# Lists of token numbers with 64 bytes for each slot, scattered and copied whole

## The chip, the cores and the metric

One core of a Trainium2 chip runs one program. The metric is the time on the device of one execution, in microseconds (us). Its engines are TensorE (PE, matmuls and transposes), VectorE (DVE), ScalarE (ACT), GpSimd (POOL) and SyncE (SP, which issues most of the transfers); PEld is TensorE's loading of weights. Transfers are carried by 16 DMA engines.

## The reference

Three layers follow one another, all in fp32:

- attention over 4 batches of 8 heads, 576 tokens, 64 wide, with keys and values averaged over groups of 8 (so 72 keys). It gives x, 2304 tokens of 512;
- a mixture of 8 experts: each token goes to the expert with the largest of 8 logits, x·w_gate. An expert takes the first 576 tokens that come to it, in order of their numbers; for those y = relu(x·w1)·w2 (512 to 1024 to 512), scaled by the softmax weight; other tokens give 0;
- a last layer for all 2304 tokens: g = s·relu(x·w_in)² + b, then g·w_out (512 to 2048 to 512).

## The kernel before, in words

**Routing.** Attention runs in tiles of up to 128 tokens, five in each batch. `route` (L296) follows behind it for a batch, or for a part of it: for each token it works out the slot (`rsi`) that the token has in its expert's part of a list, and POOL then scatters the numbers of the tokens (`tok`, from an iota, L360) into the list `ids` in DRAM, one number of 4 bytes to each slot, by an indirect DMA of up to 128 numbers for every tile (L363; 20 in all, five for a batch; those of the last batch come as three and two). `scale` (L283) stores the rows of x to the DRAM array `xd` (L294). Before the first scatter, `fill` (L841) writes `ids` and the second list, `idc`, full with a number that is out of bounds.

**Units.** The tokens are worked on in units: 288 slots of one expert each, then two small ones of 144, and the last of the big units is wide (288 and 64 more). The first two units begin while attention still runs for the last batches. For a unit u, SP reads where its slots begin (`values_load`), loads their token numbers `idt` (L809, 96 partitions of 3), then weights: `kraw` for w1 (L787) and `vraw` for w2 (L793). POOL gathers the rows of x by `idt` (L804). The weights are split in a high and a low part, since a product is made of three matmuls: ACT casts the high part (`w1h` L796, `w2h` L800), POOL or DVE subtracts for the low part (`w1l` L797, `w2l` L801). `x_part` (L811 on) transposes x on PE and splits it (`xs`, ACT L816 and DVE L817), `layer1` (L824 on) and `layer2` (L998) multiply.

**The list of results.** `store_y` (L1000) stores y of a unit to `yt`, and then copies the unit's token numbers from `idt` in SBUF into `idc` (L1004), at the place where its results lie; the small units do so from `ids_s`, and the wide one's last 64 numbers come from `idw` (L1143). When the units are done, `last_layers` (L1240) reads y and, by `load_y` (L908), the numbers `it`, works the last layer out for 256 tokens at a time and scatters the rows of the output by `it` (L1325). It begins with the cast `gh` (L1312) and the loads of `sb` (L1464), of `wo` and of `raw` (spilled weights `wi`, L932).

**What sets the order.** The program's order is written out by hand on every engine, and each engine's queue runs in order. SP issues its transfers one after the other; eight semaphores are used in turn for them, so a DMA on SP waits for the one eight before it to have landed. POOL's transfers have eight of their own. Tiles that take the place of others in SBUF wait for all that was done with those: the pools `one` (attention) and `left` (kept to the end) matter below. When attention is over, the pool `one` is given up, and the tiles of the units (`w2h` for f from 1 on among them) take its place.

Of the kernel before, what the change touches and what calls it, by code (L numbers as in the profile page):

```python
# [10 lines left out]
I32 = mybir.dt.int32  # L11
# [7 lines left out]
B, H, S, D = 4, 8, 576, 64  # L19
T = B * S  # L20
DM = H * D
E, FF, FF2 = 8, 1024, 2048
POOL = 8
SP = S // POOL
P = 128
NB = 5
VW = D + 1 + E
G = H + H // 2
BIG = 1 << 17
KSCALE = 1.0 / (POOL * 8.0)  # L30
CH = 288
SUB = 96
# [2 lines left out]
KF = FF // P  # L35
KF2 = FF2 // P
CU = 256
TINY = float(np.array([897 << 20], np.int32).view(np.float32)[0])


# [39 lines left out]
def attention(nc, tc, c, a, cap, capp, left, big, xd, ids, run, hist, first, ps0):  # L80
# [3 lines left out]
    with ExitStack() as es:  # L84
        one = es.enter_context(tc.tile_pool(name="a1", bufs=1))
# [191 lines left out]
        todo, routes, scales, at_pe = [], [], [], [None]  # L277
# [18 lines left out]
        def route(b, t0, t1):  # L296

            g, w = b % 2, t1 - t0
            l = lg[g][:, t0:t1]
            bc = lambda z: z.unsqueeze(2).to_broadcast([P, w, E])  # L300
            tmp = lambda name, shape, dt=F32: left.tile([P, NB] + shape, dt, name=f"{name}{len(routes) % 2}")[:, 0:w]
# [4 lines left out]
            d = tmp("rd", [E])  # L306
# [49 lines left out]
            yield  # L356
            si = tmp("rsi", [], I32)
            nc.vector.tensor_copy(si, sf)
            tok = tmp("tok", [], I32)
            nc.gpsimd.iota(tok, pattern=[[P, w]], base=b * S + t0 * P, channel_multiplier=1)  # L360
            for t in range(w):
                n = rows(t0 + t)
                i = nc.gpsimd.indirect_dma_start(out=ids, out_offset=bass.IndirectOffsetOnAxis(ap=si[:n, t:t + 1], axis=0),  # L363
                                                 in_=tok[:n, t:t + 1], in_offset=None, bounds_check=E * capp - 1, oob_is_err=False)
                tc.declare_no_dep(i.ins, group="scatter", reason="slots of different tokens")
                tc.add_to_no_dep_group("scatter", i.ins)
            if t1 == NB and b:
# [24 lines left out]
        o = ps1.tile([P, 2, 512], F32, name="o")  # L392
# [90 lines left out]
        while todo or scales:  # L483
            more = 7
            while more and todo:
                more -= 1
                if step():
# [3 lines left out]
                    o = ps1.tile([P, 2, 512], F32, name="o")  # L491
# [14 lines left out]
SM = CH // 2  # L506
SSUB = SM // 2
# [8 lines left out]
MORE = 64  # L516
# [237 lines left out]
class Experts:  # L754
# [51 lines left out]
                                          bounds_check=rows - 1, oob_is_err=False)  # L806

    def load_ids(self, u, slots):
        self.nc.sync.dma_start(out=self.idt[u % 3], in_=slots.rearrange("(s p) o -> p (s o)", p=SUB))  # L809

    def x_part(self, u, k, p, v=None):  # L811
        v = v or self.v
# [28 lines left out]
    def fill(self, pool):  # L841

        nc = self.nc
        for d, w in ((self.ids, E * self.capp // SUB + 1), (self.idc, (T + 2 * CH) // SUB)):
            z = pool.tile([SUB, w], I32, name=f"z{w}")
            nc.gpsimd.iota(z, pattern=[[1, w]], base=BIG, channel_multiplier=0)
            nc.sync.dma_start(out=d.rearrange("(p n) o -> p (n o)", p=SUB), in_=z)

    def beside(self, i, pool):

# [57 lines left out]
    def load_y(self, u):  # L908
        nc = self.nc
        nc.sync.dma_start(out=self.yr, in_=self.yt[:, u * CU:u * CU + CU].rearrange("(k p) n -> p k n", p=P))  # L910
        nc.sync.dma_start(out=self.it[u % 4], in_=self.idc[u * CU:u * CU + CU].rearrange("(j p) o -> p (j o)", p=P))

    def split_y(self, k, eng):
        self.nc.scalar.copy(self.yh[:, k], self.yr[:, k])
# [21 lines left out]
    def main(self, left, one, ps):  # L936
# [44 lines left out]
        regs = self.regs  # L981
# [15 lines left out]
                for i, (l, r) in enumerate(((w2h, v.hh), (w2h, v.hl), (w2l, v.hh))):  # L997
                    nc.tensor.matmul(py[d][:, :v.n], lhsT=l[f][:, d * P:d * P + P], rhs=r[f], start=f == 0 and i == 0, stop=f == KF - 1 and i == 2)  # L998

        def store_y(u, y, ids, n, sub):  # L1000
            for d in range(KD):
                nc.scalar.copy(y[:, d], py[d][:, :n])
            nc.sync.dma_start(out=self.yt.rearrange("(d p) n -> p d n", p=P)[:, :, cols(u, n)], in_=y)
            nc.sync.dma_start(out=self.idc[cols(u, ids.shape[1] * sub)].rearrange("(s p) o -> p (s o)", p=sub), in_=ids)  # L1004

        def store_unit(u, v=self.v):
            store_y(u, yo(0 if v is wide else u % 2, v.n), self.idt[u % 3], v.n, SUB)

        pos = [0]

# [8 lines left out]
        def next_tokens(u):  # L1019
            if u < NU:  # L1020
                load_regs(u, u - 2)
                self.load_ids(u, self.ids[bass.ds(regs[u][1], CH)])
                nc.sync.dma_start(out=idw[u % 3], in_=self.ids[CH:][bass.ds(regs[u][1], MORE)])

        def tokens(u, s):
            if s < NSUB:
# [73 lines left out]
        def small_ids(s):  # L1100
            if s < E:
                load_regs(sid(s), self.t.NV + s)
                nc.sync.dma_start(out=self.ids_s[s % 4], in_=self.ids[bass.ds(regs[sid(s)][1], SM)].rearrange("(s p) o -> p (s o)", p=SSUB))

        def small_gather(s):
            for j in range(2):
# [20 lines left out]
                nc.tensor.matmul(py[d][:, :SM], lhsT=self.w2r[:, f, d * P:d * P + P], rhs=hs[f], start=f == 0, stop=f == KF - 1)  # L1127

        def store_small(s):
            store_y(sid(s), yo(s % 2, SM), self.ids_s[s % 4], SM, SSUB)  # L1130

        def next_small(s):
            if s < E:
# [3 lines left out]
        def to_small(u, v=self.v, f0=0):  # L1137

            if u == 1:
                zeros()  # L1140
            small_gather(0)
            if v is wide:
                nc.sync.dma_start(out=self.idc[CH:][cols(u, MORE)], in_=idw[u % 3])  # L1143
            with if_new(self.t.NV):
                self.load_w1(w1s(sid(0)))
            small_gather(1)
            for f in range(f0, KF):
                layer2(f, v)
                if 0 <= f - max(f0, 3) < KD:
                    small_x(0, f - max(f0, 3))  # L1150
                conv(2, MARK)
                if f == max(f0, 2):
                    with if_new(self.t.NV):
                        for j in range(0, KF, 2):
                            self.load_w2(w2s(sid(0)), j)
            store_unit(u, v)
            small_layer1(MARK)
            conv(MARK - pos[0], MARK)
# [308 lines left out]

def program(nc, tc, a, cap, out):
    capp = (-(-cap // CH) + 1) * CH
    with ExitStack() as es:  # L1470
        left = es.enter_context(tc.tile_pool(name="c", bufs=1))
        dr = es.enter_context(tc.tile_pool(name="dr", bufs=1, space=DRAM))
        xd = dr.tile([T, DM], F32, name="xd")
        ids = dr.tile([E * capp + SUB, 1], I32, name="ids")
        idc = dr.tile([T + 2 * CH, 1], I32, name="idc")
        yt = dr.tile([DM, T + 2 * CU], F32, name="yt")
        wi = [dr.tile([P, DM], F32, name=f"wi{i}") for i in range(PRE)]
        hist = left.tile([P, E], F32, name="hist")
        run = left.tile([P, E], BF16, name="run")
        ps0 = es.enter_context(tc.tile_pool(name="ps0", bufs=1, space=PSUM))  # L1480
        c = constants(nc, left, capp)
        with tc.manual_schedule():
            with tc.tile_pool(name="m", bufs=1, side="right") as m:
                x = Experts(nc, tc, c, a, left, m, xd, ids, idc, yt, wi, hist, cap, capp)
                ps = attention(nc, tc, c, a, cap, capp, left, m, xd, ids, run, hist, x, ps0)
                w = es.enter_context(tc.tile_pool(name="w", bufs=1))
                pp = es.enter_context(tc.tile_pool(name="ps", bufs=1, space=PSUM))
                ps = ps + [pp.tile([P, 512], F32, name=f"bank{i}") for i in range(2, 8)]
                with tc.tile_pool(name="m1", bufs=1) as m1:
                    x.main(w, m1, ps)  # L1490
            pool = es.enter_context(tc.tile_pool(name="n", bufs=1))
            last_layers(nc, tc, c, a, pool, x, ps, out)
# [20 lines left out]
```

## Time and profile before

| | |
|---|---|
| median of 3 runs | 694.91 us (692.51 to 697.27) |
| the profiled execution | 693.31 us, its span 691.6 us |
| PE | busy 597.8 us, 86% |
| DVE | 384.4 us, 56% |
| POOL | 328.3 us, 47% |
| ACT | 253.0 us, 37% |
| mean granted TensorE clock | 0.93 of full speed |
| transfers | 67,826 packets, 86.24 MB, 30,732 of the packets under 512 bytes |

The span is the time from the first to the last instruction of the core; the rest of an execution's time lies around it. In the rows, times are in microseconds from the span's start; "x3" is a count of instructions that the view puts together, and [4.99 <-DMA kraw<-...] says that the engine stood idle for 4.99 us before the row and what ended that. DMA is the mean busy share of the 16 DMA engines, beside the bytes that they moved.

The attention stage lies at 0 to 125 us, the routing's last scatters and the first units at 110 to 175, the units up to 370, and the last layer fills the rest.

### The profile page before, as it was taken

How to read it: one execution, taken by the hardware profiler on the slowest of the kernel's cores; microseconds unless marked ns; L12 is line 12 of the kernel's file. 1: busy time of each engine (PE TensorE's matmuls, PEld its weight loads, DVE VectorE, ACT ScalarE, POOL GpSimd, SP SyncE). 2: the span in 40 equal slices, each digit the busy share in tenths (PEclk: the TensorE clock that was granted, in tenths of full speed). 3: DMA queues.
4: the chain of work that ended last, by engine and by line, in shares of the span. 5: the costliest groups of instructions: out<-in, count | busy, mean ns of one | idle time of the engine just before them, and what ended most of it. 6: DMA issues, size and time to landing. Idle time of an engine off the chain costs nothing. (4 is left out here: it accounts for less than half of the span.)

```text
span 691.6 us, 11294 instructions
## 1 busy us (share of the span) xinstructions
PE 597.8 (86%) x3943; PEld 556.4 (80%) x3943; DVE 384.4 (56%) x804; ACT 253.0 (37%) x617; POOL 328.3 (47%) x357
## 2 busy tenths in 40 slices
PE   7788887765896898977879789999979999999986
PEld 6777876665896797977769769989859989899886
DVE  4789898865698584566353769597302112022060
ACT  1354574441554362614234744403303304124040
POOL 5566743656482552734112666455253515326081
PEclk8799998996899899998789979999989999999999
DMA  8999875875448968699851910010730100100000
GB/s 171 194 180 161 139 116 168 184 243 194 57 130 161 285 133 304 130 309 254 272 119 43 363 62 1 1 31 1 267 113 17 31 32 1 46 17 2 17 18 20
DMA packets 67826, 86.24 MB, mean 125 GB/s; under 512 B 30732, under 2 KB 38924, under 8 KB 67724
## 3 DMA queue, kind: packets, MB, share of 16 engines
q1 hardware_dynamic: 59596, 63.52, 36.7%
q0 software_dynamic: 7280, 21.51, 11.9%
q8 instruction: 43, 0.70, 0.5%
q14 instruction: 59, 0.48, 0.3%
q10 hardware_dynamic: 848, 0.02, 0.1%
HBM read 66.14 MB, written 19.72 MB: 124 GB/s over the span
## 5 line engine op out<-in xcount | busy, mean ns | idle before, releaser
L1317 PE MATMUL bank<-wo,gh 128*128 128x512 f32 (+1 forms) x448 | 132.6, 380 | 1.2 <-DVE wo L1283 1.2
L1313 POOL TENSOR_TENSOR gl<-rt,gh 128x256 fp32r<-128x256 f32 (+1 forms) x112 | 90.9, 820 | 79.9 <-ACT gh L1312 76.8
L1317 PEld LDWEIGHTS bank<-wo,gh 128*128 128x128 f32 x448 | 82.5, 193 | 15.5 <-DVE wo L1283 1.5
L1317 PE MATMUL bank<-wo,gl 128*128 128x512 f32 (+1 forms) x224 | 85.4, 381 | 4.1 <-POOL gl L1313 4.1
L998 PE MATMUL bank<-hs,w2h 128*128 128x288 f32 (+1 forms) x308 | 74.5, 332 | 8.8 <-issue 8.8
L797 POOL TENSOR_TENSOR w1l<-kraw,w1h 128x512 fp32r<-128x512 f32 x40 | 53.2, 1350 | 36.8 <-ACT w1h L796 36.6
L998 PEld LDWEIGHTS bank<-hs,w2h 128*128 128x128 f32 x308 | 56.2, 212 | 9.5 <-issue 9.3
L1324 DVE SCALAR_TENSOR_TENSOR raw<-bank,sb,c_u 128x512 f32<-128x512 f32 (+1 forms) x14 | 9.8, 710 | 96.5 <-PE bank L1317 96.5
L998 PE MATMUL bank<-hs,w2l 128*128 128x288 f32 (+1 forms) x148 | 48.3, 326 | 10.9 <-POOL w2l L801 8.9
L1307 ACT ACTIVATE rt<-tq 128x256 f32<-128x256 f32 (+1 forms) x26 | 9.6, 369 | 129.1 <-PE tq L921 105.9
L1317 PEld LDWEIGHTS bank<-wo,gl 128*128 128x128 f32 x224 | 43.0, 192 | 12.4 <-POOL gl L1313 4.6
L1308 DVE SCALAR_TENSOR_TENSOR rt<-bank,rt 128x256 f32<-128x256 f32 (+1 forms) x60 | 24.3, 405 | 44.8 <-ACT rt L1307 44.6
L1325 POOL DMA_INDIRECT out_dram<-raw,it x12 | 12.1, 1004 | 71.2 <-DVE raw L1324 58.9
L1312 ACT CAST gh<-rt 128x256 fp32r<-128x256 f32 (+1 forms) x112 | 43.1, 385 | 6.6 <-DMA idc<-ids_s 5.4
L998 PEld LDWEIGHTS bank<-hs,w2l 128*128 128x128 f32 x148 | 31.6, 214 | 11.6 <-POOL w2l L801 9.2
L921 PE MATMUL bank<-yhl,w2h 128*128 128x256 f32 x208 | 38.0, 283 | 0.0
L921 PE MATMUL bank<-yhl,w1h 128*128 128x256 f32 x208 | 37.7, 281 | 0.0
L1307 ACT ACTIVATE rt<-bank 128x256 f32<-128x256 f32 (+1 forms) x60 | 22.2, 370 | 37.4 <-PE bank L921 33.4
L921 PEld LDWEIGHTS bank<-yhl,w1h 128*128 128x128 f32 x208 | 32.3, 188 | 1.0 <-issue 0.7
L921 PEld LDWEIGHTS bank<-yhl,w2h 128*128 128x128 f32 x208 | 32.7, 191 | 0.3
L801 DVE TENSOR_TENSOR w2l<-vraw,w2h 128x512 fp32r<-128x512 f32 x39 | 28.2, 723 | 3.3 <-ACT w2h L800 2.7
L921 PE MATMUL bank<-yhl,w1l 128*128 128x256 f32 x104 | 29.3, 282 | 0.6 <-issue 0.6
(376 smaller groups left out, 1592.6 us busy)
## 6 DMA issues: line engine op xcount, KB each, us to landing
kraw<-in_moe_w_dram SPq DMA_DIRECT2D x12, 1024.0 KB
vraw<-in_moe_w_dram SPq DMA_DIRECT2D x16, 512.0 KB
c_raw<-in_moe_w_in_dram POOLq DMA_DIRECT2D x16, 512.0 KB, 9.0
kraw<-in_k_dram SPq DMA_DIRECT2D x8, 576.0 KB
out_dram<-c_u SPq DMA_DIRECT2D x1, 4608.0 KB
q<-in_q_dram SPq DMA_DIRECT2D x16, 256.0 KB
xd<-xr SPq DMA_DIRECT2D x16, 256.0 KB
vraw<-in_moe_w_dram SPq DMA_DIRECT2D x4, 1024.0 KB
```

The lines of the kernel that those rows point to most:

```text
L797: eng.tensor_sub(self.w1l[:, i], self.w1(i), self.w1h[:, i])
L801: eng.tensor_sub(self.w2l[i], self.w2r[:, i], self.w2h[i])
L921: self.nc.tensor.matmul(p[:, :CU], lhsT=l[:, k], rhs=r[:, k], start=n == 0, stop=n == 3 * KD - 1)
L998: nc.tensor.matmul(py[d][:, :v.n], lhsT=l[f][:, d * P:d * P + P], rhs=r[f], start=f == 0 and i == 0, stop=f == KF - 1 and i == 2)
L1307: nc.scalar.activation(r, p, AF.Relu)
L1308: nc.vector.scalar_tensor_tensor(out=r, in0=p, scalar=0.0, in1=r, op0=ALU.max, op1=ALU.mult)
L1312: nc.scalar.copy(gh[:, f, :n], rt[f % 4][:, :n])
L1313: nc.gpsimd.tensor_sub(gl[:, f, :n], rt[f % 4][:, :n], gh[:, f, :n])
L1317: nc.tensor.matmul(p[:, c], lhsT=l[:, f, j * P:j * P + P], rhs=wo[f][:, z, c], start=f == 0 and i == 0, stop=f == KF2 - 1 and i == 2)
L1324: nc.vector.scalar_tensor_tensor(out=o[:, c], in0=p[:, c], scalar=sb[:, 0:1], in1=sums["drop"][:, c], op0=ALU.mult, op1=ALU.add)
L1325: i = nc.gpsimd.indirect_dma_start(out=dst, out_offset=bass.IndirectOffsetOnAxis(ap=ids, axis=0), in_=o[:, c], in_offset=None, bounds_chec ...
```

## The change

`ids` and `idc` become arrays with a row of 16 numbers, 64 bytes, for each slot (`ROW`). The iota writes each token's number 16 times over, the scatter copies whole rows of 64 bytes, and whoever reads the numbers into SBUF takes the first of each row. The list arrays are rounded up to a multiple of 768 rows, so `ids` has 7680 rows of 64 bytes (it had 7008 numbers of 4 bytes) and `idc` has 3072 (it had 2880 numbers); `fill` writes both with one tile of 96 x 128 numbers. The copy of a unit's numbers no longer starts from `idt`, `ids_s` or `idw` in SBUF: it goes from `ids` to `idc` in DRAM, in one run without gaps (`store_ids`). And `tok` is taken from the pool `one` instead of `left`.

```
+ROW = 16
...
-            tok = tmp("tok", [], I32)
-            nc.gpsimd.iota(tok, pattern=[[P, w]], base=b * S + t0 * P, channel_multiplier=1)
+            tok = one.tile([P, NB, ROW], I32, name=f"tok{len(routes) % 2}")[:, 0:w]
+            nc.gpsimd.iota(tok, pattern=[[P, w], [0, ROW]], base=b * S + t0 * P, channel_multiplier=1)
             for t in range(w):
                 n = rows(t0 + t)
                 i = nc.gpsimd.indirect_dma_start(out=ids, out_offset=bass.IndirectOffsetOnAxis(ap=si[:n, t:t + 1], axis=0),
-                                                 in_=tok[:n, t:t + 1], in_offset=None, bounds_check=E * capp - 1, oob_is_err=False)
+                                                 in_=tok[:n, t], in_offset=None, bounds_check=E * capp - 1, oob_is_err=False)
...
     def load_ids(self, u, slots):
-        self.nc.sync.dma_start(out=self.idt[u % 3], in_=slots.rearrange("(s p) o -> p (s o)", p=SUB))
+        self.nc.sync.dma_start(out=self.idt[u % 3], in_=slots[:, 0:1].rearrange("(s p) o -> p (s o)", p=SUB))
...
-        for d, w in ((self.ids, E * self.capp // SUB + 1), (self.idc, (T + 2 * CH) // SUB)):
-            z = pool.tile([SUB, w], I32, name=f"z{w}")
-            nc.gpsimd.iota(z, pattern=[[1, w]], base=BIG, channel_multiplier=0)
-            nc.sync.dma_start(out=d.rearrange("(p n) o -> p (n o)", p=SUB), in_=z)
+        z = pool.tile([SUB, 8 * ROW], I32, name="z")
+        nc.gpsimd.iota(z, pattern=[[0, 8 * ROW]], base=BIG, channel_multiplier=0)
+        for d in (self.ids, self.idc):
+            d = d.rearrange("(p n k) o -> p n (k o)", p=SUB, k=8)
+            nc.sync.dma_start(out=d, in_=z.unsqueeze(1).to_broadcast(list(d.shape)))
...
-        nc.sync.dma_start(out=self.it[u % 4], in_=self.idc[u * CU:u * CU + CU].rearrange("(j p) o -> p (j o)", p=P))
+        nc.sync.dma_start(out=self.it[u % 4], in_=self.idc[u * CU:u * CU + CU, 0:1].rearrange("(j p) o -> p (j o)", p=P))
...
-        def store_y(u, y, ids, n, sub):
+        def store_ids(u, n, i=0):
+            row = lambda z: z.rearrange("(a n) o -> a (n o)", a=1)
+            nc.sync.dma_start(out=row(self.idc[i:][cols(u, n)]), in_=row(self.ids[i:][bass.ds(regs[u][1], n)]))
+
+        def store_y(u, y, n, slots):
             for d in range(KD):
                 nc.scalar.copy(y[:, d], py[d][:, :n])
             nc.sync.dma_start(out=self.yt.rearrange("(d p) n -> p d n", p=P)[:, :, cols(u, n)], in_=y)
-            nc.sync.dma_start(out=self.idc[cols(u, ids.shape[1] * sub)].rearrange("(s p) o -> p (s o)", p=sub), in_=ids)
+            store_ids(u, slots)
...
             if v is wide:
-                nc.sync.dma_start(out=self.idc[CH:][cols(u, MORE)], in_=idw[u % 3])
+                store_ids(u, MORE, CH)
...
-        ids = dr.tile([E * capp + SUB, 1], I32, name="ids")
-        idc = dr.tile([T + 2 * CH, 1], I32, name="idc")
+        ids = dr.tile([up(E * capp + SUB), ROW], I32, name="ids")
+        idc = dr.tile([up(T + 2 * CH), ROW], I32, name="idc")
```

No engine's order changes, but for one iota less in `fill` and a few instructions that work out addresses; shapes and waits do. Two places show it. The first is SP behind the loads for unit 2 and at the end of unit 0; `idt_163` are unit 2's numbers, `idw` the further 64 that a wide unit would take. Before:

```order
L809 DMA idt_163<-ids 96x3x1 [waits DMAHW5_49,DMASW4_49]
L1023 ISA
L1023 DMA idw_1877<-ids 64x1 [waits DMAHW6_49,PE_49]
L1003 REGISTER_ALU
L1003 DMA yt<-yo 128x4x288 [waits DMAHW7_49,Activation_49]
L1004 REGISTER_ALU
L1004 DMA idc<-idt_161 96x3x1 [waits DMAHW0_49]
```

With the change:

```order
L810 DMA idt_163<-ids 96x3x1 [waits DMAHW5_49,DMASW4_49]
L1031 ISA
L1031 DMA idw_1875<-ids 64x1 [waits DMASW5_49,DMASW3_49,DMASW6_49,DMASW2_49,DMASW7_49,DMASW1_49,DMAHW6_49,DMASW0_49,PE_49]
L1011 REGISTER_ALU
L1011 DMA yt<-yo 128x4x288 [waits DMAHW7_49,Activation_49]
L1006 ISA
L1006 DMA idc<-ids 16x288 [waits DMAHW0_49]
```

The copy stands where it stood, as 16 rows of 288 numbers instead of 96 partitions of 3, and it reads the list `ids` and no tile of SBUF. The load of `idw` now also waits for POOL's transfers (DMASW0 to 7).

The second place is ACT at the end of unit 0's first layer, where `w2h` of the units' own tiles is cast for the first time. Before:

```order
L826 ACTIVATE hs<-tq 128x288 [waits PE_49]
L826 ACTIVATE hs<-misc 128x288 [waits PE_49]
L800 CAST w2h<-vraw 128x512 [waits DMAHW4_49,DMAHW3_49,DMAHW5_49,DMAHW2_49,DMAHW6_49,DMAHW0_49,DMAHW7_49,DVE_49,Activation_49]
L800 CAST w2h<-vraw 128x512 x2
L796 CAST w1h<-kraw 128x512 [waits DMAHW7_49,Pool_49]
```

With the change:

```order
L827 ACTIVATE hs<-tq 128x288 [waits PE_49]
L827 ACTIVATE hs<-misc 128x288 [waits PE_49]
L801 CAST w2h<-vraw 128x512 [waits DMASW6_49,DMASW7_49,DMASW5_49,DMAHW0_49,DMASW4_49,DMAHW2_49,DMASW3_49,DMAHW3_49,DMASW2_49,DMAHW4_49,DMASW1_49,DMAHW5_49,DMASW0_49,DMAHW6_49,DVE_49,DMAHW7_49,Activation_49,Pool_49]
L801 CAST w2h<-vraw 128x512 x2
L797 CAST w1h<-kraw 128x512 [waits DMAHW7_49]
```

The first cast of `w2h` waited for transfers of SP's queue (the DMAHW semaphores: stores of x out of the same place in SBUF); it now waits for all eight of POOL's (DMASW) and for POOL itself too, since `tok` lies in the pool whose place the tile takes. These transfers are the scatters, the last of which stand on POOL ahead of the first `w2l` (L801).

## Rows read from the trace of the kernel before

**Rows 1.** The page, part 1: busy time, share of the span, instructions.

```profile
PE 597.8 (86%) x3943; PEld 556.4 (80%) x3943; DVE 384.4 (56%) x804; ACT 253.0 (37%) x617; POOL 328.3 (47%) x357
```

**Rows 2.** The chain that ended last: start, length, what; its first long piece.

```profile
401.37 2.28 POOL yhl L915 x2
```

**Rows 3.** SP's waits: line, releaser, us in total, times, longest.

```profile
SPq L809 <- DMA ids<-tok,rsi: 17.8, 2, 11.9
...
SPq L809 <- DMA idc<-idt: 7.9, 2, 4.3
...
SPq L1143 <- DMA idc<-idt: 7.4, 1, 7.4
...
SPq L1464 <- DMA idc<-ids_s: 4.1, 1, 4.1
```

**Rows 4.** Tiles ids (scatters of numbers), then it (scatters of output rows of 2 KB).

```profile
DMA to landing us min/median/max: 5.6/10.0/15.3
...
DMA to landing us min/median/max: 2.7/2.8/4.7
```

**Rows 5.** Windows: length, busy time of engines, PE clock, DMA share, GB/s.

```profile
36.00:40.00 4.00, 2.77 (x16) 2.54 (x17) 3.61 (x9) 2.94 (x7) 1.15 (x1) 0.75 1.10 140
210.00:218.00 8.00, 7.88 (x59) 7.88 (x60) 5.13 (x11) 4.63 (x11) 2.26 (x3) 1.00 1.08 97
372.00:376.00 4.00, 3.37 (x29) 3.28 (x29) 0.00 (x0) 0.00 (x0) 0.00 (x0) 1.00 0.00 0
```

**Rows 6.** POOL's timeline, 96 to 176: start, length, line, operation, idle before.

```profile
98.90 0.92 POOL L363 DMA_INDIRECT ids<-tok,rsi  x1 [0.30 <-issue]
...
128.52 0.91 POOL L363 DMA_INDIRECT ids<-tok,rsi  x1 [0.30 <-issue]
...
144.27 0.99 POOL L804 DMA_INDIRECT xg<-xd,idt  x1 [9.83 <-DMA idt<-ids]
...
156.76 0.92 POOL L363 DMA_INDIRECT ids<-tok,rsi  x1 [0.31 <-issue]
```

**Rows 7.** SP's timeline, 96 to 176 and 280 to 330.

```profile
110.70 0.37 SPq L809 DMA_DIRECT2D idt<-ids  x1
...
141.35 0.35 SPq L809 DMA_DIRECT2D idt<-ids  x1
...
293.33 1.16 SPq L787 DMA_DIRECT2D kraw<-in_moe_w_dram  x2
```

**Rows 8.** ACT's timeline, 96 to 176 and 344 to 408.

```profile
116.64 1.14 ACT L796 CAST w1h<-kraw 128x512 fp32r<-128x512 f32 x2 [4.99 <-DMA kraw<-in_moe_w_dram]
...
147.04 1.66 ACT L800 CAST w2h<-vraw 128x512 fp32r<-128x512 f32 x3 [1.65 <-DMA xd<-xr]
...
376.35 0.41 ACT L1312 CAST gh<-rt 128x256 fp32r<-128x256 f32 x1 [5.43 <-DMA idc<-ids_s]
```

**Rows 9.** PE's timeline, around the four waits that the text speaks of.

```profile
119.28 0.46 PE L243 MATMUL te<-ident,s 64*128 64x64 f32 x4 [3.90 <-ACT eT L246]
...
159.28 0.61 PE L998 MATMUL bank<-hs,w2l 128*128 128x288 f32 x1 [8.93 <-POOL w2l L801]
...
310.73 0.34 PE L1114 MATMUL tq<-ident,xg 72*128 72x72 f32 x2 [3.82 <-DVE yr L1115]
...
399.49 0.58 PE L921 MATMUL tq<-yhl,w1h 128*128 128x256 f32 x1 [4.65 <-ACT yhl L914]
```

**Rows 10.** DVE's timeline, at five places.

```profile
128.92 5.55 DVE L325 TENSOR_SCALAR rgs<-rgs 128x3 f32<-128x3 f32 x1
...
147.75 0.69 DVE L801 TENSOR_TENSOR w2l<-vraw,w2h 128x512 fp32r<-128x512 f32 x1 [1.86 <-ACT w2h L800]
...
155.22 0.16 DVE L650 TENSOR_TENSOR u_key<-u_oth,u_e 128x8 f32<-128x8 f32 x1
...
163.00 0.46 DVE L817 TENSOR_TENSOR xs<-misc,xs 128x288 fp32r<-128x288 f32 x1 [7.62 <-ACT xs L816]
...
308.57 0.43 DVE L740 TENSOR_SCALAR c_f<-c_raw 128x512 int32<-128x512 int32 x1 [6.41 <-DMA wi<-c_f]
```

More of the change, by code (lines that the diff above doesn't have):

```diff
@@ L1003, in store_y @@
             nc.sync.dma_start(out=self.yt.rearrange("(d p) n -> p d n", p=P)[:, :, cols(u, n)], in_=y)
-            nc.sync.dma_start(out=self.idc[cols(u, ids.shape[1] * sub)].rearrange("(s p) o -> p (s o)", p=sub), in_=ids)
+            store_ids(u, slots)
         def store_unit(u, v=self.v):
-            store_y(u, yo(0 if v is wide else u % 2, v.n), self.idt[u % 3], v.n, SUB)
+            store_y(u, yo(0 if v is wide else u % 2, v.n), v.n, CH)
         pos = [0]
@@ L1022, in next_tokens @@
                 self.load_ids(u, self.ids[bass.ds(regs[u][1], CH)])
-                nc.sync.dma_start(out=idw[u % 3], in_=self.ids[CH:][bass.ds(regs[u][1], MORE)])
+                nc.sync.dma_start(out=idw[u % 3], in_=self.ids[CH:][bass.ds(regs[u][1], MORE)][:, 0:1])
         def tokens(u, s):
@@ L1102, in small_ids @@
                 load_regs(sid(s), self.t.NV + s)
-                nc.sync.dma_start(out=self.ids_s[s % 4], in_=self.ids[bass.ds(regs[sid(s)][1], SM)].rearrange("(s p) o -> p (s o)", p=SSUB))
+                nc.sync.dma_start(out=self.ids_s[s % 4], in_=self.ids[bass.ds(regs[sid(s)][1], SM)][:, 0:1].rearrange("(s p) o -> p (s o)", p=SSUB))
         def small_gather(s):
@@ L1129, in store_small @@
         def store_small(s):
-            store_y(sid(s), yo(s % 2, SM), self.ids_s[s % 4], SM, SSUB)
+            store_y(sid(s), yo(s % 2, SM), SM, SM)
         def next_small(s):
@@ L1469, in program @@
     capp = (-(-cap // CH) + 1) * CH
+    up = lambda n: -(-n // (8 * SUB)) * 8 * SUB
     with ExitStack() as es:
```

## The prediction

> **What bounds the kernel now.** I began with the busy times. PE is busy for 597.8 us of the 691.6 [rows 1], so it is the bound wherever nothing holds it up, and the change takes no matmul away. A gain can only come out of PE's waits. The chain of waits, read second, says how far to look: its first long piece is POOL's `yhl` at 401.37 [rows 2], and what comes after is the last layer on PE. So the question is how much earlier the units reach 401.
>
> Third, SP's waits, since SP issues the weights in order and whatever holds it holds them. Four of its entries belong to the two lists [rows 3]: 17.8 us in two waits for scatters to land, 7.9 and 7.4 for an earlier copy into `idc`, 4.1 for the last such copy.
>
> Fourth, why these wait so long. A scatter of 128 numbers of 4 bytes needs 10.0 us at the median until it has landed, 15.3 at most; one of 128 output rows of 2 KB, issued by POOL in the same way, 2.8 [rows 4]. The one that moves fewer bytes is over three times slower. In the windows, 210 to 218 lies inside such a copy into `idc`: the DMA engines are busy throughout (share 1.08) and move 97 GB/s [rows 5], so small writes hold up the other transfers too.
>
> Fifth, the timelines, for what follows on each wait:
>
> - Batch 1's last scatter ends its issue at 98.90 + 0.92 = 99.82 [rows 6], and `idt` is loaded at 110.70 [rows 7]: 10.9 us. Weights queue behind it; ACT waits 4.99 for them [rows 8], and behind ACT PE 3.90 [rows 9].
> - Batch 2's ends at 129.43 [rows 6], `idt` for unit 1 is loaded at 141.35 [rows 7]: 11.9 us. POOL stands still for 9.83 before its gather at 144.27, and in its order the last scatters come after that; the last one ends at 157.68 [rows 6]. `w2l` is behind it, and PE waits 8.93 us for that, until 159.28 [rows 9]. The transposes behind give DVE its `xs` at 163.00, after 7.62 us of idling [rows 10].
> - The wide unit: SP's 7.4 us end in `kraw` at 293.33 [rows 7]. DVE waits 6.41 for a store to land and PE 3.82 behind it, until 310.73 [rows 10, 9].
> - The end of the units: from 372 to 376 the DMA engines move nothing [rows 5]; ACT's first `gh` waits 5.43 for the last copy to `idc` [rows 8], SP's load of `sb` 4.1 [rows 3]. PE pays later, with 4.65 at 399.49 [rows 9].
>
> **The change, part by part.**
>
> *Scatters of 64 bytes.* The same 20 DMAs, issued in about 1 us each as now. No row shows a write of 64 bytes. The ends are 2.8 us (2 KB rows) and 10.0 (4 bytes). I take 4 us, near the lower end: the two rows differ only in the size of a row, more bytes take less time there, so what is paid for is the small write, and 64 bytes are sixteen times the slow one.
>
> The first stage gives up to 3.90 (PE's wait); I pass 3.5 on to all that comes after. The second `idt` load then comes 3.5 + (11.9 - 4.9) = 10.5 earlier (4 to land, 0.9 until SP goes on), at 130.9. The gather follows 2.9 us behind it, as now (144.27 - 141.35), at 133.8. From the gather to the end of the last scatter POOL needs 157.68 - 144.27 = 13.4: 147.2, and that has landed at 151.2.
>
> *The new wait.* ACT's first `w2h` of the units' own tiles now waits for that landing. Today it starts at 147.04 [rows 8], so here the change takes back: 151.2 is 4.2 later. Behind it on ACT are two more casts, then `w1h`; POOL's `w2l` needs them, and PE the `w2l`. DVE's `w2l` starts 0.71 after ACT's cast (147.75), and DVE needs 155.38 - 147.75 = 7.6 us to finish what lies before `xs` [rows 10]. So `xs` comes 0.7 + 7.6 = 8.3 after ACT's cast: 159.5 instead of 163.00, and DVE, not POOL, is late next. The stretch up to 175 gives 3.5 us, where PE's two waits alone would have promised 12.8. Bounds: 0, and 8.93 if DVE's table work is overtaken too.
>
> *The copies.* Now: 288 writes of 4 bytes each. With the change: 16 runs of 1152 bytes in DRAM. No row shows a copy inside DRAM; the ends are 2.8 and 10.0 again [rows 4], and I take 3, since 1152 bytes are nearest to the 2 KB row. SP's 7.4 then goes and `kraw` comes 7.4 earlier; the spill's store, which DVE waits for, no longer queues behind those loads. PE's 3.82 bounds it: I take 2.5. Where the other copies are followed by loads, PE has no wait for weights that I could name, and I count nothing; PE's own work hides them.
>
> *The end of the units.* SP's 4.1 and ACT's 5.43 go: the casts no longer wait for a store that reads a tile whose place they take. Loads start 4 us earlier, and the stretch behind them waits for loads; I take 4, between 0 and 5.43.
>
> *The fill.* 7680 and 3072 rows of 64 bytes are 688,128 bytes instead of 39,552. At the 140 GB/s of 36 to 40 [rows 5] that is 4.6 us more on engines that are fully busy then. Ends 0 and 4.6. I take 1: only loads for later tiles queue behind it.
>
> *At no cost:* readers still fetch single numbers of 4 bytes, as many as before; an iota writes 80 numbers a partition instead of 5 and runs on POOL while scatters wait; the extra address instructions on SP precede DMAs that no engine awaits.
>
> Sum: -3.5 - 2.5 - 4 + 1 = -9.0. The profiled execution's 693.31 becomes 684.3. It lies 1.6 below the median of the runs, 694.91, so I say **686**. About 1% (6.95 us) is what a measurement of this kernel can tell from no change.
>
> **The rivals.**
>
> *Writes of 64 bytes land as slowly as those of 4* (slower). Then nothing shortens the chain up to the last scatter at 157.68, it lands at 167.7, and the new wait holds ACT until then. `xs` follows at 176.0 instead of 163.00: +13.0. The copies, in longer runs, still give 2.5 + 4, the fill takes 1: 694.9 + 13.0 - 6.5 + 1 = 702.4, and up to 706 if the fill costs its 4.6. It decides from the point where the last scatter lands after 163.0 - 8.3 = 154.7; as the landing enters the sum about 2.7 times ((167.7 - 151.2)/(10 - 4)), that is a landing of 5.3 us, a little below the fastest of today's, 5.6 [rows 4]. For it: the new wait is certain. Against it: the step from 10.0 to 2.8. The Trainium skill (DMA: Bandwidth & Descriptors, Specifications) says that transfers below 512 bytes are done by read-modify-write, which would put 64 bytes with the 4; by that rule the time would be this rival's. The rows bear the rule out at 4 bytes only. Chance 0.13.
>
> *The new wait eats the stage's gain* (no change). A landing near 5.3 us, or POOL's subtractions slowing DVE (DVE's L325, on 128 x 3 numbers, took 5.55 us at 128.92 [rows 10]), leaves 0 up to 175; the wide unit's 2.5 may then be hidden by DVE's own work. With 4 from the end and 1 for the fill: 692. Chance 0.25.
>
> *More than I count* (larger gain). PE's whole 8.93 goes, 3.82 and 5.43 too, and the fill is free: 694.9 - 18.2 = 677. For it: the share of 1.08 at 97 GB/s shows that the small writes stall transfers that I count at nothing. Against it: the new wait, and DVE next. Chance 0.14.
>
> **How the numbers follow.** My forecast keeps 0.48. Its bounds run from 680 to 692 (landing 3 to 5 us, each smaller term from a half to its whole). To leave out no more than 2 in 10, the range goes on over the no-change case and a part of both outer ones: 675 to 698. Faster by over 1% (below 688) is most of the forecast and the larger gain: 0.41 + 0.14 = 0.55. Slower by over 1% (above 701.9) is the upper part of the first rival: 0.09. The rest, 0.36, is no change.
>
> **What would show it.** In the profile after: scatters landing in about 4 us; SP's waits for `ids<-tok` at a third of 17.8; ACT's first own `w2h` released by a DMA of `ids`, near 151; DVE's `xs` near 159.5; no waits of SP for `idc`; `gh` without its 5.43; and the chain's first `yhl` near 392. The forecast is wrong if 64-byte scatters land above 5.3 us, if the copy within DRAM takes as long as the old one, or if PE's waits come back at other places before 401.

## The result, and the profile after

The changed kernel takes 674.55 us (median of 5 runs, 669.13 to 679.57), the kernel before 694.91 (5 runs, 692.51 to 697.62): a ratio of 0.968 with a 95% interval of 0.962 to 0.974. That is 20 us less, where I had forecast 9, and just below the range. Executions of a kernel show a faster and a slower state: medians here and below are of all runs, ratios of those in the faster state alone. The profiled execution took 676.53 us with a span of 674.8, so between the two profiles the gain is 16.8.

PE's busy time has fallen by 6.6 us against [rows 1], at as many matmuls and a mean granted clock of 0.937 instead of 0.930. So about 10 of the 16.8 us come out of its waits, and the rest from busy time, of which the prediction had nothing:

```profile
PE 591.2 (88%) x3943; PEld 550.9 (82%) x3943; DVE 387.5 (57%) x804; ACT 252.7 (37%) x617; POOL 327.6 (49%) x356
```

The chain that ended last begins (start, length, what) with the same piece as in [rows 2], 16 us earlier:

```profile
385.34 3.15 POOL yhl L917 x3
```

SP's waits (line, releaser, total, times, longest) that answer to [rows 3]: 3.2 us are left of 17.8 for the scatters. For copies into `idc`, 1.6 us are left.

```profile
SPq L810 <- DMA ids<-tok,rsi: 3.2, 1, 3.2
...
SPq L1006 <- DMA idc<-ids: 1.6, 1, 1.6
```

Before, those were 29.1 us, since to the three entries of [rows 3] belong two more, which the prediction passed over:

```profile
SPq L1103 <- DMA idc<-ids_s: 7.7, 1, 7.7
...
SPq L787 <- DMA idc<-idt: 2.0, 1, 2.0
```

The scatters land in 5.4 us at the median, against 10.0 in [rows 4]:

```profile
DMA to landing us min/median/max: 2.0/5.4/9.5
```

POOL's timeline (start, length, line, operation, idle before), for [rows 6]:

```profile
98.47 0.92 POOL L364 DMA_INDIRECT ids<-tok,rsi  x1 [0.30 <-issue]
...
124.09 0.92 POOL L364 DMA_INDIRECT ids<-tok,rsi  x1 [0.30 <-issue]
...
131.48 1.00 POOL L805 DMA_INDIRECT xg<-xd,idt  x1 [1.29 <-issue]
...
143.38 0.92 POOL L364 DMA_INDIRECT ids<-tok,rsi  x1 [0.30 <-issue]
...
149.73 0.32 POOL L1245 MEMSET rt<- 128x256 f32 x1 [5.43 <-DMA ids<-tok,rsi]
```

SP's, for [rows 7]:

```profile
104.41 0.38 SPq L810 DMA_DIRECT2D idt<-ids  x1
...
128.86 0.36 SPq L810 DMA_DIRECT2D idt<-ids  x1
...
278.56 1.13 SPq L788 DMA_DIRECT2D kraw<-in_moe_w_dram  x2
```

Batch 1's scatters end their issue at 99.39 and `idt` is loaded at 104.41: 5.0 us instead of 10.9. Batch 2's end at 125.01, `idt` is loaded at 128.86: 3.9 instead of 11.9. The last scatter ends at 144.30, 13.4 us earlier. Then POOL stands still for 5.43 us until the scatters have landed, and ACT for 9.72, which is the new wait. ACT's timeline, for [rows 8]:

```profile
149.72 1.66 ACT L801 CAST w2h<-vraw 128x512 fp32r<-128x512 f32 x3 [9.72 <-DMA kraw<-in_moe_w_dram]
...
358.44 0.41 ACT L1320 CAST gh<-rt 128x256 fp32r<-128x256 f32 x1 [0.79 <-DMA idc<-ids]
```

The view names `kraw` as what ended the wait, a load with which POOL's row does not agree: it resumes at the same time, 149.73, and names `ids`. Of several semaphores the view shows one. At the end of the units `gh` now waits 0.79 instead of 5.43.

DVE's `xs`, which was to come at 159.5, comes at 163.09, no earlier than the 163.00 of [rows 10]. The rows ahead of it show why, operations on 128 x 8 numbers that take 1.3 us:

```profile
150.98 1.26 DVE L599 TENSOR_TENSOR u_left<-hist,u_taken 128x8 f32<-128x8 f32 x1
...
152.16 1.32 DVE L601 TENSOR_SCALAR u_oth<-u_ie,u_f 128x8 f32<-128x8 f32 x1
...
163.09 0.45 DVE L818 TENSOR_TENSOR xs<-misc,xs 128x288 fp32r<-128x288 f32 x1
```

The same two in the kernel before, from DVE's timeline there, took 0.16 and 0.23:

```profile
148.36 0.16 DVE L598 TENSOR_TENSOR u_left<-hist,u_taken 128x8 f32<-128x8 f32 x1
...
148.44 0.23 DVE L600 TENSOR_SCALAR u_oth<-u_ie,u_f 128x8 f32<-128x8 f32 x1
```

In between POOL subtracts; before, it was still scattering then:

```profile
150.94 1.28 POOL L802 TENSOR_TENSOR w2l<-vraw,w2h 128x512 fp32r<-128x512 f32 x1 [0.89 <-ACT w2h L801]
152.17 3.77 POOL L798 TENSOR_TENSOR w1l<-kraw,w1h 128x512 fp32r<-128x512 f32 x3
```

From its first `w2l` to the end of the table in front of `xs` DVE needs 12.7 us (150.37 to 163.09) instead of 7.6. All six of these small operations that take over 0.9 us lie beside POOL's subtractions (150.94 to 155.94 and 158.66 to 161.32). That is what ate the stretch's gain, as far as times can show it; no run separates the two.

The window behind the same copy into `idc` (length, busy time of PE, PEld, DVE, ACT, POOL, PE clock, DMA share, GB/s). It begins 1.8 us after the copy's issue, as 210 to 218 did before, where 97 GB/s were moved [rows 5]:

```profile
209.00:217.00 8.00, 8.00 (x42) 8.00 (x42) 3.45 (x6) 2.97 (x7) 1.82 (x2) 0.63 0.88 305
```

To see where the time went, I take three instructions of PE, at the same place in its order in both kernels. Two of them in the kernel before, PE's timeline:

```profile
174.70 0.74 PE L815 MATMUL tq<-ident,xg 96*128 96x96 f32 x3 [5.97 <-DVE xs L817]
...
401.42 0.58 PE L921 MATMUL tq<-yhl,w1h 128*128 128x256 f32 x1 [1.35 <-POOL yhl L915]
```

and after:

```profile
172.62 0.74 PE L816 MATMUL tq<-ident,xg 96*128 96x96 f32 x3 [5.39 <-DVE xs L818]
...
298.09 0.35 PE L1122 MATMUL tq<-ident,xg 72*128 72x72 f32 x2 [0.59 <-DVE yr L1123]
...
385.39 0.58 PE L923 MATMUL tq<-yhl,w1h 128*128 128x256 f32 x1 [3.35 <-POOL yhl L917]
```

The first is the first transpose behind the table of units, the last one the last layer's start, from which PE runs on. The one between them stands in [rows 9] at 310.73, behind a wait of 3.82 that is 0.59 now. So the time divides (us), the last column being the prediction's:

| stretch | before | after | gain | forecast |
|---|---|---|---|---|
| start to 174.70, with the fill | 174.70 | 172.62 | 2.1 | 3.5 - 1 |
| 174.70 to 310.73, units and wide unit | 136.0 | 125.5 | 10.6 | 2.5 |
| 310.73 to 401.42, small units and end | 90.7 | 87.3 | 3.4 | 4 |
| from 401.42 to the last matmul | 283.8 | 283.2 | 0.6 | 0 |

The stretch of the units and the wide unit gave four times what I had counted. PE's waits show where. Before, there were three that end in no event that the profile shows ("issue"), from 221.8 to 262.5. Their 10.7 us are the size of the stretch's gain:

```profile
PE bank L998 <- issue: 10.7, 3, 4.5
```

and after (line numbers are two higher):

```profile
PE bank L1000 <- issue: 0.2, 1, 0.2
```

Two of the three (4.49 and 4.34 us) lie in a branch of PE, the one that asks whether another unit follows. Such a branch took up to 6.96 us before and takes up to 0.44 now (duration in ns, minimum, median, maximum):

```profile
L1208 PEldq COMPARE_BRANCH  x3: 882/6451/6956, 188.4 to 255.6; - x3
...
L1216 PEldq COMPARE_BRANCH  x3: 359/390/437, 187.0 to 252.4; - x3
```

The other engines' branches are as short before as after, each under 0.1 us at this line. The third wait (1.86 us at 235.10) has no branch.

In the small units such waits did not fall:

```profile
PE bank L1127 <- issue: 5.0, 1, 5.0
...
PE bank L1135 <- issue: 7.5, 2, 4.0
```

PE is idle there for 20.1 us before and 20.9 after. The 3.4 us of that stretch are PE's busy time, 70.6 and 66.4 us, at a granted clock of 0.86 and 0.90.

### The profile page after: what moved, and what is told of

It reads as the page before. It is cut to its first block, busy times and chain, and to the rows that moved or that the text cites. A ratio compares the mean times of both kernels' runs of the same rounds, so it can differ in the third digit from the quotient of the medians.

```text
span 674.8 us, 11312 instructions
## 1 busy us (share of the span) xinstructions
PE 591.2 (88%) x3943; PEld 550.9 (82%) x3943; DVE 387.5 (57%) x804; ACT 252.7 (37%) x617; POOL 327.6 (49%) x356
## 5 line engine op out<-in xcount | busy, mean ns | idle before, releaser
L1325 PEld LDWEIGHTS bank<-wo,gh 128*128 128x128 f32 x448 | 81.8, 191 | 13.9
L1000 PE MATMUL bank<-hs,w2h 128*128 128x288 f32 (+1 forms) x308 | 71.6, 321 | 7.8 <-ACT w2h L801 7.7
L798 POOL TENSOR_TENSOR w1l<-kraw,w1h 128x512 fp32r<-128x512 f32 x40 | 52.5, 1333 | 31.5 <-ACT w1h L797 31.1
L1000 PEld LDWEIGHTS bank<-hs,w2h 128*128 128x128 f32 x308 | 53.6, 203 | 8.5 <-ACT w2h L801 7.9
L1325 PEld LDWEIGHTS bank<-wo,gl 128*128 128x128 f32 x224 | 42.8, 191 | 12.4 <-POOL gl L1321 4.5
L1000 PE MATMUL bank<-hs,w2l 128*128 128x288 f32 (+1 forms) x148 | 46.7, 315 | 0.0
L802 DVE TENSOR_TENSOR w2l<-vraw,w2h 128x512 fp32r<-128x512 f32 x39 | 27.3, 699 | 10.6 <-ACT w2h L801 9.9
L825 PE MATMUL bank<-xs,w1h 128*128 128x288 f32 (+1 forms) x120 | 28.4, 320 | 4.3 <-DVE xs L818 4.3
L1000 PEld LDWEIGHTS bank<-hs,w2l 128*128 128x128 f32 x148 | 30.0, 203 | 0.2 <-DVE w2l L802 0.2
```

What stands on the lines that cost most here:

```text
L798: eng.tensor_sub(self.w1l[:, i], self.w1(i), self.w1h[:, i])
L802: eng.tensor_sub(self.w2l[i], self.w2r[:, i], self.w2h[i])
L825: self.nc.tensor.matmul(p, lhsT=l[:, f, k], rhs=r[k], start=n == 0, stop=n == 3 * KD - 1)
L1325: nc.tensor.matmul(p[:, c], lhsT=l[:, f, j * P:j * P + P], rhs=wo[f][:, z, c], start=f == 0 and i == 0, stop=f == KF2 - 1 and i == 2)
```

## The experiments

The time of one kernel varies by some 10 us from run to run, and much of that arises in attention, where these kernels do nearly the same: PE's L255 that starts at 102.73 in the kernel before comes between 99.9 and 107.6 in the others. So beside the times I give two stretches of each profiled execution, from PE's instructions above and that one: **A**, from L255 to the first transpose behind the table (72.0 us before, 70.3 after), and **B**, from that transpose to the last layer's start (226.7 before, 212.8 after). Both come from a single execution of each kernel. Ratios are to the kernel before on the same chip, with their 95% intervals.

**The copies alone.** The lists and the scatters of the kernel before, and only this:

```
-            nc.sync.dma_start(out=self.idc[cols(u, ids.shape[1] * sub)].rearrange("(s p) o -> p (s o)", p=sub), in_=ids)
+            store_ids(u, slots)
```

> Slots of 4 bytes and the scatters as before; only the copies into idc are changed (list to list in one run, 16 pieces of 72 bytes). If the copies carry what I left out of the sum (the units from 200 to 282, the wide unit, the end), this takes most of the 20 us: 678 to 683, with PE's three waits between 220 and 263 (10.7 us in sum, put down to issue) gone or small, and the stretch up to 175 as before. If the scatters carry it, 690 or more and the three waits stay.

Measured: 675.61 us, ratio 0.971 (0.965 to 0.977). PE's two instructions:

```profile
180.22 0.74 PE L815 MATMUL tq<-ident,xg 96*128 96x96 f32 x3 [6.35 <-DVE xs L817]
...
389.81 0.58 PE L921 MATMUL tq<-yhl,w1h 128*128 128x256 f32 x1 [3.35 <-POOL yhl L915]
```

A is 72.6 (from 107.61), as before; B is 209.6, so 17 us shorter. The copies alone give a gain that can't be told from that of the whole change.

**The scatters alone.** The changed kernel, with the copies from SBUF again, each number to a row of 64 bytes:

```
-            store_ids(u, slots)
+            nc.sync.dma_start(out=self.idc[cols(u, ids.shape[1] * sub), 0:1].rearrange("(s p) o -> p (s o)", p=sub), in_=ids)
```

> The change without its copies: rows of 64 bytes, scattered whole, tok in the pool one; but idc is written from idt in SBUF, 4 bytes to each row of 64. If the copies carry the gain: 690 to 694, only the stretch up to 175 some 2 to 3 us shorter, PE's three issue waits between 220 and 263 still there, SP's 7.4 us ahead of the wide unit's last copy and ACT's 5 us at gh too. If the scatters carry it: 680 or less.

Measured: 679.87 us, ratio 0.969 (0.962 to 0.977); A 71.1, B 215.1, from an execution of 683.40 us. The number is the one set for the scatters, but after the run ahead of it that can't be the reason: the copies alone had given as much. With the run of 16 pieces undone the gain stays. But this kernel does not have the old copies back. Its 288 writes are of 4 bytes still, but no longer side by side. So the next question was whether it is the size of a write or its neighbours.

**Copies spaced, nothing else.** The kernel before; only `idc` has a row of 64 bytes for each number (its fill and its reader follow):

```
-        idc = dr.tile([T + 2 * CH, 1], I32, name="idc")
+        idc = dr.tile([up(T + 2 * CH), ROW], I32, name="idc")
-            nc.sync.dma_start(out=self.idc[cols(u, ids.shape[1] * sub)].rearrange("(s p) o -> p (s o)", p=sub), in_=ids)
+            nc.sync.dma_start(out=self.idc[cols(u, ids.shape[1] * sub), 0:1].rearrange("(s p) o -> p (s o)", p=sub), in_=ids)
```

> The kernel before, scatters and ids as they were, and the copies still from SBUF with 4 bytes for each number; only idc has a row of 64 bytes for each, so that no two of these writes touch the same 64 bytes. If it is the closeness of the small writes that makes them slow: 675 to 681, as with the copies in one run. If it is their size: 692 to 697, as before.

Measured: 679.95 us, ratio 0.975 (0.970 to 0.981); A 72.3, B 211.7. As many writes of as few bytes from the same tile, and 15 us of B are gone. The scatters, which I had not touched, land as slowly as ever:

```profile
DMA to landing us min/median/max: 10.6/12.4/16.1
```

**Scatters spaced.** The changed kernel, but each scatter writes only the first 4 bytes of a row, and `tok` is small again and lies in `left`, so the new wait is gone too:

```
-            nc.vector.tensor_copy(si, sf)
-            tok = one.tile([P, NB, ROW], I32, name=f"tok{len(routes) % 2}")[:, 0:w]
+            nc.vector.tensor_scalar(out=si, in0=sf, scalar1=float(ROW), scalar2=None, op0=ALU.mult)
+            tok = tmp("tok", [], I32)
...
-                i = nc.gpsimd.indirect_dma_start(out=ids, out_offset=bass.IndirectOffsetOnAxis(ap=si[:n, t:t + 1], axis=0),
-                                                 in_=tok[:n, t], in_offset=None, bounds_check=E * capp - 1, oob_is_err=False)
+                i = nc.gpsimd.indirect_dma_start(out=ids.rearrange("a (b o) -> (a b) o", o=1), out_offset=bass.IndirectOffsetOnAxis(ap=si[:n, t:t + 1], axis=0),
+                                                 in_=tok[:n, t:t + 1], in_offset=None, bounds_check=(E * capp - 1) * ROW, oob_is_err=False)
```

> The changed kernel, its rows of 64 bytes kept, but each scatter writes only the first 4 bytes of a row (indices times 16), and tok, small again, lies in the pool left, so the new wait is gone too. If closeness makes small writes slow: the numbers land as fast as the changed kernel's, SP waits 2 to 4 us for ids, 668 to 674. If size does: they land in some 10 us, SP waits 14 to 18 us for them, 676 to 682 (only the copies gain).

Measured: 668.28 us (665.09 to 669.92), ratio 0.959 (0.954 to 0.963); A 66.0, B 212.8.

```profile
DMA to landing us min/median/max: 2.1/6.2/9.8
```

Numbers of 4 bytes, spaced, land in 6.2 us, near the 5.4 of rows of 64 bytes and not the 10.0 to 12.4 of numbers side by side. For the landing, spacing decides, not size. By its median this is also the fastest kernel of the study; the changed kernel, run again beside it, took 673.01, but its runs (663.64 to 678.67) overlap with these, and its ratio is the same.

> The changed kernel once more, beside the others on this chip: 672 to 677.

It was 673.01 us, ratio 0.959 (0.951 to 0.967), A 70.6, B 208.2. So B varies by some 5 us between executions of one kernel.

**How close is close.** Rows of 32 and of 16 bytes in the changed kernel (`ROW = 8`, `ROW = 4`), written whole:

> The changed kernel with rows of 32 bytes for each slot, so that two slots share 64 bytes. If sharing of 64 bytes is what makes writes slow, its scatters land later than the changed kernel's median of 5.4 us, toward 10, and SP waits over 8 us for them: 675 to 682. If 32 bytes are enough: as the changed kernel, 671 to 677, landing near 5 us.

> The same with rows of 16 bytes, four slots to 64 bytes: by sharing of 64 bytes still slower, 678 to 690 (the new wait follows the scatters' landing); if 32 bytes are the border, this one is slow and the kernel ahead of it is not.

Measured: 674.90 us, ratio 0.970 (0.965 to 0.975), and 673.55, ratio 0.966 (0.961 to 0.972); B 208.6 and 205.7. With rows of 16 bytes:

```profile
DMA to landing us min/median/max: 4.4/5.1/5.8
```

Both expectations of something slower fell: four slots may share 64 bytes without harm. What is slow lies below rows of 16 bytes; 8 I did not try.

**The copies twice.** The kernel before, every copy in `store_y` issued twice:

```
             nc.sync.dma_start(out=self.idc[cols(u, ids.shape[1] * sub)].rearrange("(s p) o -> p (s o)", p=sub), in_=ids)
+            nc.sync.dma_start(out=self.idc[cols(u, ids.shape[1] * sub)].rearrange("(s p) o -> p (s o)", p=sub), in_=ids)
```

> The kernel before, with every copy from SBUF into idc issued twice, the same numbers to the same places. If the copies cost the 15 to 20 us that the changed kernel got back: 705 to 715. If I mistake what the units got back, and the copies lie beside other work as the prediction had it: up to 699.

Measured: 733.35 us, ratio 1.045 (1.038 to 1.052). By the medians it is 37 us, by the ratio 31, more than I expected. The profile (of an execution of 734.61 us) shows that SP waits for each first copy to land before it issues the second:

```profile
SPq L1005 <- DMA idc<-idt: 43.7, 5, 9.8
...
SPq L1005 <- DMA idc<-ids_s: 23.1, 2, 16.1
```

That is 66.8 us for seven copies, 9.5 each, and the program takes 4.5 to 5.3 longer for each. The copies do not lie beside other work. But here SP's wait and the writes themselves come together, and this run does not separate them.

**Who pays: SP's queue, or all transfers.** Beside each copy of the changed kernel a transfer that nobody reads, on ACT's queue, first close, then spaced:

```
             store_ids(u, slots)
+            nc.scalar.dma_start(out=self.junk.rearrange("(s p) o -> p (s o)", p=SUB), in_=self.c.ident[:SUB, 0:3])
...
+        junk = dr.tile([CH, 1], F32, name="junk")
```

> The changed kernel, and beside each of its copies a transfer that nobody reads, issued on ACT's queue: 288 numbers of 4 bytes from SBUF, close together, into a small array of its own in DRAM. It is to be held against the next kernel. If the old copies cost what they did because close small writes hold up all other transfers (weights, instructions), whoever issues them: 8 to 18 us above the next kernel. If they cost through SP's own waits for them: at most 3 us above it.

> The same transfer that nobody reads on ACT's queue, but each of its 288 numbers goes to a row of 64 bytes of its own. It shows what the additional DMA costs by its issue and its place in the queue: 672 to 678, close to the changed kernel, by either theory.

Measured: 696.31 us (ratio 0.999, 0.996 to 1.003) and 680.06 (0.978, 0.974 to 0.983). Between the two lie 16 us (15 by the ratios); B is 226.1 and 207.6. Nobody reads these numbers, and still close writes took back most of the gain. PE is idle for 39.1 and 23.7 us in B, and that difference is the one between its waits that end in "issue" (19.0 and 3.5 us in all). Close:

```profile
PE bank L1136 <- issue: 13.9, 2, 7.3
PE bank L923 <- issue: 4.5, 1, 4.5
PE bank L1000 <- issue: 0.6, 1, 0.6
```

Spaced:

```profile
PE bank L1136 <- issue: 3.5, 1, 3.5
```

So the price falls on the same kind of wait as in the kernel before, but at other places: of the 18.5 us between the two Bs, 16.0 lie in the small units and the end, and only 2.5 in the units. SP's own waits are not wholly out of it: those that name `idc` grew from 5.8 to 15.2 us; the ACT queue's DMAs use the eight semaphores of SP's turn. The window around the second of these writes, close and then spaced:

```profile
211.00:219.00 8.00, 8.00 (x58) 8.00 (x57) 3.92 (x9) 5.17 (x12) 4.42 (x5) 0.92 0.81 87
```

```profile
211.00:219.00 8.00, 7.50 (x57) 7.27 (x56) 5.61 (x10) 4.03 (x10) 3.75 (x4) 1.00 0.74 216
```

87 GB/s against 216: the other transfers crawl while 288 close numbers are written. The spaced write is issued 2 us earlier (211.07 against 213.09), so set to the writes the windows are 214 to 222 and 212 to 220: 113 against 245 GB/s. The spaced one's median lies some 6 us above the changed kernel's, more than I had allowed for. Where these go isn't shown: SP waits 4.2 us at a `kraw` that in the changed kernel hasn't this wait, but it issues that load no later behind the copy (7.8 us against 8.2).

**The new wait.** First without it: the changed kernel with `tok` in `left` again (`rd` and `rde` of `route` go to `one` for room):

```
-            tok = one.tile([P, NB, ROW], I32, name=f"tok{len(routes) % 2}")[:, 0:w]
+            tok = tmp("tok", [ROW], I32)
```

> The changed kernel with tok back in the pool left (two small tiles of route, rd and rde, go to the pool one to make room), so ACT's first own w2h waits for no scatter. If the new wait is what keeps the stretch up to 175 from its gain: w2h starts at 140 to 143 instead of 149.7, the table on DVE ends 4 to 8 us earlier, and the time is 667 to 671. If DVE and POOL, or the transfers of weights, hold that stretch anyway: 673 to 676, as the changed kernel.

Measured: 673.57 us, ratio 0.966 (0.959 to 0.972); A 67.2, B 210.8. In A it is 3 us faster than the changed kernel (70.3, 70.6), and the spaced scatters, which lack the wait as well, 4 to 5 (66.0). The seven profiled executions that have both the wait and scatters set apart lie at 69.7 to 72.8. In the time the difference can't be told from the run-to-run scatter. ACT does not start when I thought it would (44.6 us behind L255, against 47.4 in the changed kernel); another DMA is late next, the store of x out of the same place:

```profile
149.36 1.66 ACT L801 CAST w2h<-vraw 128x512 fp32r<-128x512 f32 x3 [6.57 <-DMA xd<-xr]
```

Then the wait by itself: the kernel before with `tok` in `one`.

```
-            tok = tmp("tok", [], I32)
+            tok = one.tile([P, NB], I32, name=f"tok{len(routes) % 2}")[:, 0:w]
```

> The kernel before, with only tok moved into the pool one: the new wait beside scatters of 4 bytes that land as slowly as before. By the prediction's sum for its slow rival the wait costs 13 us: w2h starts near 167 instead of 147, DVE's xs near 176, and the time is 705 to 710. If weights or DVE hold that stretch anyway, 697 to 701.

Measured: 706.29 us, ratio 1.011 (1.006 to 1.017), 10 us above the 696.42 of the kernel before on this chip (8 by the ratio); A 81.2, 9.2 longer.

```profile
163.48 1.66 ACT L800 CAST w2h<-vraw 128x512 fp32r<-128x512 f32 x3 [15.93 <-DMA ids<-tok,rsi]
```

The mechanism of my slow rival was real: with scatters that land slowly, this wait alone makes the kernel slower.

## Why the prediction was wrong

**The step that failed** is the price of the copies in the units. The prediction says: "Where the other copies are followed by loads, PE has no wait for weights that I could name, and I count nothing; PE's own work hides them." With the 2.5 us for the wide unit and the 4 for the end I had 6.5 for all copies; B fell by 13.9 between the two profiles, and over nine profiled executions without close copies (205.7 to 212.8, mean 209.8) by 17. A tenth, of the scatters alone, had 215.1, in an execution of 683.40 us. The copies alone gave 17, doubling them cost 31 to 37 us of time, and close writes beside the new copies cost 15 to 16 again.

I had the row for it: share 1.08 at 97 GB/s, inside a copy [rows 5]. The prediction read it ("so small writes hold up the other transfers too"), but priced the copy by SP's waits for it, and passed over two of these. The copy's larger price is paid by others: for some 10 us everything else that is on its way moves at a third of its pace or less (97 GB/s against 305 in the like window, and 52 from 211 to 221).

What came late for PE was not weights, for which it has no wait there, but, by the trace's times, its own code. In the kernel before, a 16 KB transfer of the queue that the profile calls "instruction" (q8) starts at 223.66 and ends at 224.67, inside PE's branch from 219.25 to 226.20. In the changed kernel the like transfer ends at 218.23, before PE reaches the branch at 220.58, and the branch takes 0.36. In all fourteen profiles such a transfer ends 1.2 to 1.6 us before the end of every branch over 0.8 us that PE has in the units, 43 in all. And it starts later with close writes under way: 13.4 and 13.1 us behind PE's hints at the first two such branches (BRANCH_PREFETCH_HINT, at 210.23 and 246.60) in the kernel before, 8.3 and 6.7 in the changed one; 11.2 and 9.4 with the close write beside, 6.9 and 6.7 with the spaced one. PE's branches in the units, the small ones among them, take 24.7 to 31.1 us in the four kernels with close copies or close writes beside, and 10.5 to 13.7 in the ten others. The prediction has no term for these branches.

Point by point:

- **Scatters.** 4 us from issue to landing was a little low: the 5.4 is just above the 5.3 that the prediction named as a sign of being wrong, where this stage's gain ends. The two loads of `idt` come 5.0 and 3.9 us behind the last scatter, where I said 4.9, so what hangs on them came about as forecast.
- **The new wait.** ACT's cast came at 149.72, forecast 151.2, and the wait does take back 3 to 5 us, as the two kernels without it show in A. Right.
- **DVE next.** Right in kind, wrong in size: `xs` at 163.09, not 159.5, since DVE's table slowed beside POOL's subtractions, which I had in a rival, at a chance of 0.25. The stretch gave 2.1 us instead of 3.5 less the fill.
- **The wide unit and the end.** `kraw` came at 278.56 instead of 293.33, and PE's 3.82 are 0.59. `gh` waits 0.79 instead of 5.43. But the 3.4 us of the small units and the end only look like the forecast 4: PE's idle time did not fall in that stretch of this profile (20.1 and 20.9), as it now waits 5.1 us for a gather and 2.5 more for "issue". The gain there is busy time at a higher granted clock. The number was luck.
- **The fill.** I took 1 us; PE's instruction at 102.73 comes at 102.30 now. Not visible.
- **The slow rival.** Its mechanism is shown, at 8 to 10 us for the 13 that I worked out. Its condition was not met: writes of 64 bytes do not land as those of 4. The Trainium skill (DMA: Bandwidth & Descriptors, Specifications) says that transfers below 512 bytes are done by read-modify-write; here writes of 16 and of 64 bytes, both below, land in 5.1 and 5.4 us, and spaced ones of 4 in 6.2, so the rule as I used it did not tell slow from fast.
- **More than I count**, 677, was the nearest case, at 0.14. Its sum does not hold: PE still waits 7.65 us for `w2h`, where it let the whole 8.93 go. But its argument, that small writes stall transfers that I count at nothing, is what the runs bore out.
- **Waits that come back**, the prediction's last sign of being wrong: they did, before 401, with the gather's 5.1 us, and with 7.7 for DVE's `xs` in the units, where it had been 3.3 (both besides the wait at the first transpose).

The change's own idea holds only in part: neither the 64 bytes nor the copy in one run is needed. To move the numbers of `idc` apart is enough for the copies, and to move those of `ids` apart is enough for the scatters' landing. Spaced scatters beside close copies I did not run, so what they give alone in time is not measured.

Open is why writes side by side are slow. Open, too, is why a code transfer starts so late behind its hint: that close writes delay it is shown by the kernels with and without them, but not at which point it is held. The wait of 1.86 us without a branch has no cause shown, nor has the rise of the granted clock in the small units. And the place of the loss depends on when PE reaches its branches: in the kernel with close writes beside, two branches in the units take 2.45 and 2.19 us, but PE comes to them later and waits 0.6.

## What to carry to other kernels

Where a window shows the DMA engines busy throughout at a fraction of their usual GB/s, find the transfer that does this and price it as time lost to all others that are on their way, not by the waits that name it; issue it twice, or an idle twin beside it, to measure. Where a wait of TensorE ends in "issue", look for a branch there and for the transfer of its code. A list of single numbers in DRAM that are written one by one gets a row of at least 16 bytes for each (rows of 16 were written whole; single numbers were tried at 64 bytes apart). And a tile moved to a pool that is given up while its transfers are under way makes the next tenant wait for them: price that by the slowest landing, as here, where it cost 8 to 10 us with scatters of numbers side by side and 3 to 5 with rows of 64 bytes.

## What I had not expected of the hardware

- 288 writes of 4 bytes, side by side in DRAM, hold up the core's other transfers while they last: 87 to 97 GB/s at a DMA share of 0.8 to 1.1, against 216 to 305 in like windows without them.
- Such writes cost TensorE time in its branches: up to 6.96 us in the kernel before for one that takes 0.44 at most in the changed one, and a 16 KB transfer of code ends inside it.
- The same 4 bytes at a pitch of 64 bytes do no such harm, nor do rows of 16 or 32 bytes side by side. Landing at the median: 10.0 and 12.4 us for 4 bytes side by side, 6.2 spaced, 5.1 for rows of 16, 5.4 for rows of 64.
